# Six of eight experts taken in order of their load, each place with a capacity of its own

## The chip, the cores and the metric

One core of a Trainium2 chip. The metric is the device time of one execution in microseconds (us); lower is better. The kernel before takes 831.09 us in the median of three runs (829.47 to 831.78). About 0.3% of that, 2.5 us, is what a measurement of this kernel can tell from no change.

Engines are named as the profile names them: PE (TensorE; PEld is its weight load), DVE (VectorE), ACT (ScalarE), POOL (GpSimd) and SP (SyncE, whose queue issues most DMAs).

## What is computed

Three steps, each fed by the one before, all in float32:

```python
x = attention(q, k, v)              # 4 batches, 8 heads, 576 positions, 64 wide: a local window of 7
                                    # positions plus attention over means of 4; as rows: x is 2304 x 512
x = (silu(x @ w_gate) * (x @ w_val)) @ w_out        # hidden width 1536
xn, en = x / |x|, expert_emb / |expert_emb|
logits = xn @ en.T / tau                            # 8 experts
idx = argmax(logits, axis=1)                        # one expert for each row
out[idx == e] = gate[idx == e] * (relu(x[idx == e] @ w1[e]) @ w2[e])    # w1[e] 512 x 1024, w2[e] 1024 x 512
```

The last step is ragged: how many of the 2304 rows an expert gets is known only on the chip, when the last rows have been routed. For the input of the reference the eight counts are 297, 284, 329, 305, 296, 231, 280, 282.

## The kernel before, in words

**Products.** A float32 operand is split in two parts of a narrower float type (fp32r), hi and lo, and a product is three matmuls: hi by hi, hi by lo, lo by hi. ACT casts the hi part, DVE (now and then POOL) subtracts to get the lo part.

**Stages.** 16 pairs of heads (`heads`) feed the gated step, which runs over nine chunks of 256 rows (`gated`, `gemm1`, `gemm1p`, `gemm2`, `gemm2p`). The result rows go to a table in DRAM, `x2d`, and are routed chunk by chunk (`route`, `route_rows`, the last chunk in `last_m`): each row gets a slot number in its expert's stretch of two small tables `tabs`, which hold row number, gate and target. `base` holds the running counts. Behind the last chunk `last_base` works out whether an expert got more rows than its capacity.

**Experts.** They are taken in the order 0 to 7. Every expert has 336 columns (`CAP`, the sum of the tiles `SLT` = 128, 128 and 80 rows): the rows in its slots are gathered from `x2d` into three tiles (`load_slots` for experts 0 to 2, `load_groups` for the others), turned so that rows become columns, and padded with zeros. The first product (`l1`, line 1789) streams all 336 columns of an expert past the weights, 96 matmuls; the second one of experts 1 to 6 (`block_t`, line 1895) does the same, another 96, and `turn_out` (line 1855) turns the result back. The second product of expert 7 (`second`, `l2`, line 1799) goes tile by tile: for each of its three tiles 24 matmuls of 512 columns. Expert 0 begins early with two tiles (256 columns) and does its third one later (`rest_a`, `rest_b`). `send` and `finish` scatter the rows to `out`. Weights come in 64 loads of 512 KB on SP's queue (`load_experts`, lines 1604 and 1607) into a ring of 36 slots; ACT casts each (line 1587) and DVE subtracts (line 1590).

**Rows past a capacity.** Behind the last expert stands a branch on a register that is read from `ovm` (line 2105). Only if an expert got more than 336 rows are the rest computed there, tile by tile (`past_tile`).

**What sets the order.** All of it is listed by a planner (`Sched`): tasks ask for an engine with a duration and a priority, the lowest number first, and the planner writes each engine's instructions in the order in which it imagines them. On the chip each engine runs its list in order and waits by semaphores. The numbers are constants at the head of the file: `HEAD_P`, `REST_P`, `HALF_P` and others for the head pairs, `WEIGHT_P` and `PART_P` for the weights of the gated step, `LAT_DMA` for the time that the planner gives a DMA.

**The start.** Until the first chunk is there, `keep_warm` (line 432) fills PE with products of zeros, as many as the planner sees room for.

Of the kernel before, what the change touches and what calls it, by code (L numbers as in the profile page):

```python
# [30 lines left out]
E = 8  # L31
# [22 lines left out]
NCST = P + P // 2 + NPAIR * WK // 2 + 3 * E + 4 * NT18 + NOV  # L54
NEYE = P + P // 2
DMA_T = 700.0
NX = 3
# [22 lines left out]
def t_actp(n): return 65 + 0.815 * n  # L80
# [22 lines left out]
class Sched:  # L103
# [7 lines left out]
    LAT_DMA = 4302.0  # L111
# [154 lines left out]
HEAD_P = [-2.213, -0.549, -1.68, -1.811, 3.298, 3.164, 2.209, 4.92, 16.0, 17.0, 18.0, 19.0, 36.0, 37.0, 38.0, 39.0]  # L266
# [5 lines left out]
REST_P = [0.035, -0.34, 0.132, 3.049]  # L272
HALF_P = [0.772, -3.481, 2.169, -0.88]
VALUE_P = 1.076
PART_P = [-0.491, 0.188, 0.558]
CONST_P = 4.124
TAB_P = 14.361
EN_P = 0.664
# [7 lines left out]
WEIGHT_P = [1.117, 2.258, 4.696, 6.055, -10.334, 12.398]  # L286


def build(tc, a):
# [66 lines left out]
    past = take(NOV)  # L356
    tri = cst.tile([P, P], F32R, name="tri")
# [9 lines left out]
    ovm = cst.tile([P, 1], I32, name="ovm")  # L367

# [656 lines left out]
    def x_pair(c, k, xh, xl):  # L1025
        hi = -0.4
# [27 lines left out]
    def act_h(c, p, ps, j):  # L1054
# [3 lines left out]
        yield op("ACT", t_actp(CT), -0.5)  # L1058
        nc.scalar.activation(th, ps[:, 0:CT], AF.Tanh, scale=0.5)
        yield op("DVE", t_dve(CT), -0.5)  # L1060
        nc.vector.scalar_tensor_tensor(out=th, in0=th, scalar=1.0, in1=ps[:, 0:CT], op0=ALU.add, op1=ALU.mult)
        yield op("DVE", t_dve(CT), -0.5)
        nc.vector.scalar_tensor_tensor(out=th, in0=th, scalar=0.5, in1=ps[:, CT:2 * CT], op0=ALU.mult, op1=ALU.mult)  # L1063
        sc.put("ps", ps)
        yield op("ACT", t_act(CT), -0.5)
        nc.scalar.copy(hh[:, j].bitcast(F32R), th)  # L1066
        e = yield both(CT, -0.5)
# [50 lines left out]
    def act_half(c, u, i, pg, pv, hh, hl):  # L1118
# [4 lines left out]
        yield op("ACT", t_actp(CT), -0.5)  # L1123
        nc.scalar.activation(th, pg[:, r], AF.Tanh, scale=0.5)  # L1124
        yield op("DVE", t_dve(CT), -0.5)
# [6 lines left out]
        yield op("DVE", t_dve(CT), -0.5)  # L1132
# [5 lines left out]
        yield op("ACT", t_act(CT), -0.5)  # L1138
        nc.scalar.copy(hf, th)  # L1139
        e = yield both(CT, -0.5)  # L1140
# [263 lines left out]
    def last_base():  # L1404
        yield op("DVE", 75, -0.9, True)
        nc.vector.tensor_tensor(out=base, in0=base, in1=base0, op=ALU.subtract)
        yield op("DVE", 80, -0.9)
        nc.vector.tensor_reduce(out=ovc, in_=base, axis=AX.X, op=ALU.max)
        yield op("DVE", 75, -0.9)
        nc.vector.tensor_scalar(out=ovc, in0=ovc, scalar1=float(CAP), scalar2=0.0, op0=ALU.subtract, op1=ALU.max)  # L1410
        yield op("DVE", 75, -0.9)
        nc.vector.tensor_copy(ovm, ovc)

    def route_rows(c, m, row, lp):
# [9 lines left out]
        for e in range(NFIRST if c in FIRST_C else 0, E):  # L1424
            yield op("DVE", t_dve(DM) + 10, -0.3, "acc")
# [257 lines left out]
    def load_groups(e):  # L1683

        if e > 3:
            yield ("wait", ("xs", e - 2, 0))
# [536 lines left out]
```

## Time and profile before

| | |
|---|---|
| median of three runs | 831.09 us (829.47 to 831.78) |
| the profiled execution | 830.24 us, its span 828.4 us |
| PE busy | 816.2 us (99%) |
| DVE, ACT, POOL busy | 562.0, 372.6, 209.6 us |
| HBM read and written | 86.10 and 10.89 MB |

The span runs from the first to the last instruction; 1.84 us of the execution's own time lie around it. "Busy" of PE counts an instruction from its start to a modelled end, and the next one starts before that end: the time that a matmul costs in a row of them is the distance between two starts, not its duration. An engine's row of idle time names what ended it.

### The profile page before, as it was taken

To read this page: it belongs to the slowest core of one execution; us is meant where nothing else is said; L and a number is where in the kernel's file an instruction comes from. 1 tells how busy PE (TensorE), PEld (TensorE's weight loads), DVE (VectorE), ACT (ScalarE), POOL (GpSimd) and SP (SyncE) were. 2 spreads that over 40 slices of the span, in tenths; PEclk is the share of its full clock that TensorE was granted. 3 is DMA by queue.
4 is the path that set the end of the run, shared out by engine and by line. 5 is a ranking of instruction groups with operands and counts; after the bars stand their busy time and mean duration, and the time that the engine had idled before them with its cause. 6 is when DMAs were issued, how large, how long until landed. Compare 5 with 4: busy or idle time off the path is not lost. (4 is left out here: it accounts for less than half of the span.)

```text
span 828.4 us, 16139 instructions
## 1 busy us (share of the span) xinstructions
PE 816.2 (99%) x6155; PEld 715.9 (86%) x6161; DVE 562.0 (68%) x1450; ACT 372.6 (45%) x923; POOL 209.6 (25%) x221
## 2 busy tenths in 40 slices
PE   9989999999999999999999999999999999999997
PEld 5778778877787787787899999999999999999995
DVE  6999989678545577544699985766467675774510
ACT  3988788453223443223422323355346464454331
POOL 5562200010000100000123230123344734744111
PEclk9999999999999999999999999999999999999999
DMA  9983546222120230110432100454476555555100
GB/s 264 321 259 107 167 151 197 94 101 61 60 60 3 83 123 13 61 60 2 152 77 27 53 1 27 118 184 109 135 239 193 178 166 173 186 168 170 49 29 30
DMA packets 64049, 96.34 MB, mean 116 GB/s; under 512 B 14753, under 2 KB 33699, under 8 KB 63840
## 3 DMA queue, kind: packets, MB, share of 16 engines
q1 hardware_dynamic: 58688, 85.50, 33.5%
q0 software_dynamic: 4992, 9.51, 3.6%
q8 instruction: 49, 0.80, 0.4%
q14 instruction: 32, 0.26, 0.1%
q10 hardware_dynamic: 288, 0.26, 0.1%
HBM read 86.10 MB, written 10.89 MB: 117 GB/s over the span
## 5 line engine op out<-in xcount | busy, mean ns | idle before, releaser
L1165 PE MATMUL ps<-xb,w 128*128 128x512 f32 x512 | 173.6, 400 | 0.0
L1109 PE MATMUL ps<-xb,w 128*128 128x256 f32 x960 | 126.9, 284 | 0.0
L1789 PE MATMUL ps<-xh,w 128*128 128x336 f32 (+1 forms) x512 | 124.8, 316 | 0.5 <-issue 0.4
L1109 PEld LDWEIGHTS ps<-xb,w 128*128 128x128 f32 x960 | 121.4, 191 | 1.4 <-issue 0.2
L1165 PEld LDWEIGHTS ps<-xb,w 128*128 128x128 f32 x512 | 96.1, 188 | 22.6 <-issue 0.8
L1165 PE MATMUL ps<-xl,w 128*128 128x512 f32 x256 | 100.6, 393 | 0.0
L1789 PEld LDWEIGHTS ps<-xh,w 128*128 128x128 f32 x512 | 88.5, 188 | 2.2 <-DVE xl L1752 1.2
L1590 DVE TENSOR_TENSOR w<-w,w 128x1024 fp32r<-128x1024 f32 x64 | 77.1, 1219 | 10.2 <-ACT w L1587 7.4
L1789 PE MATMUL ps<-xl,w 128*128 128x336 f32 (+1 forms) x256 | 79.8, 312 | 0.0
L1775 DVE SCALAR_TENSOR_TENSOR el<-ps,eh 128x336 fp32r<-128x336 f32 (+1 forms) x62 | 30.0, 493 | 64.6 <-ACT eh L1773 60.1
L1730 POOL DMA_INDIRECT xs<-x2d,w x55 | 65.7, 1194 | 22.6 <-issue 14.9
L1773 ACT ACTIVATE eh<-ps 128x336 fp32r<-128x336 f32 (+1 forms) x62 | 27.7, 447 | 96.7 <-PE ps L1789 69.8
L1587 ACT CAST w<-w 128x1024 fp32r<-128x1024 f32 x64 | 65.9, 1049 | 0.0
L1165 PEld LDWEIGHTS ps<-xl,w 128*128 128x128 f32 x256 | 48.2, 188 | 8.5
L1895 PE MATMUL x<-eh,w 128*128 128x336 f32 x192 | 51.4, 317 | 0.0
L1895 PE MATMUL ps<-eh,w 128*128 128x336 f32 x192 | 51.3, 317 | 0.0
L1227 PE MATMUL x<-w,hh 128*128 128x512 f32 x160 | 50.4, 396 | 0.0
L1789 PEld LDWEIGHTS ps<-xl,w 128*128 128x128 f32 x256 | 48.3, 189 | 0.1
L1139 ACT CAST hh<-th 128x256 fp32r<-128x256 f32 x64 | 24.0, 408 | 41.4 <-DVE th L1133 41.3
L1126 DVE SCALAR_TENSOR_TENSOR th<-th,ps 128x256 f32<-128x256 f32 x64 | 23.9, 415 | 27.3 <-ACT th L1124 27.3
L1066 ACT CAST hh<-th 128x256 fp32r<-128x256 f32 x44 | 17.8, 406 | 52.8 <-DVE th L1063 52.3
L1197 PE MATMUL x<-w,hh 128*128 128x512 f32 x128 | 41.0, 401 | 0.0
(337 smaller groups left out, 1725.9 us busy)
## 6 DMA issues: line engine op xcount, KB each, us to landing
w<-w SPq DMA_DIRECT2D x64, 512.0 KB
w<-w_gate SPq DMA_DIRECT2D x10, 512.0 KB
w<-w_val SPq DMA_DIRECT2D x10, 512.0 KB
w<-w_out SPq DMA_DIRECT2D x10, 512.0 KB
aw<-qk SPq DMA_DIRECT2D x16, 291.0 KB
x2d<-sg SPq DMA_DIRECT2D x18, 256.0 KB
w<-qk SPq DMA_DIRECT2D x12, 291.0 KB
xl<-x2d SPq DMA_DIRECT2D x13, 256.0 KB
```

The lines of the kernel that those rows point to most:

```text
L1109: nc.tensor.matmul(ps[:, o:o + CT], ww[:, k, fs], xx[:, k, :], start=(k == 0 and n == 0), stop=(k == KD - 1 and n == 2))
L1139: nc.scalar.copy(hf, th)
L1165: nc.tensor.matmul(ps, ww[:, k, fs], xx[:, :, k], start=(k == 0 and n == 0), stop=(k == KD - 1 and n == 2))
L1197: nc.tensor.matmul(x2p[x], l, r[:, js], start=(u == 0 and n == 0), stop=(u == 2 * NFB - 1 and n == 2))
L1227: nc.tensor.matmul(x2p[c, m], l[:, j, ms], r[:, js], start=(p == 0 and j == 0 and n == 0), stop=(p == NFB - 1 and j == 1 and n == 2))
L1587: nc.scalar.copy(hi.bitcast(F32R), raw)
L1590: nc.vector.tensor_tensor(out=lo.bitcast(F32R), in0=raw, in1=hi.bitcast(F32R), op=ALU.subtract)
L1730: nc.gpsimd.indirect_dma_start(out=xs[:, n * P:(n + 1) * P], out_offset=None, in_=x2d.rearrange("t (a d) -> (t a) d", a=KD), in_offset=bas ...
L1773: nc.scalar.activation(hh[:, j, 0:n].bitcast(F32R), ps[:, 0:n], AF.Relu)
L1775: nc.vector.scalar_tensor_tensor(out=hl[:, j, 0:n].bitcast(F32R), in0=ps[:, 0:n], scalar=0.0, in1=hh[:, j, 0:n].bitcast(F32R), op0=ALU.max ...
L1789: nc.tensor.matmul(ps[:, 0:n], ww[:, k, fs], xx[:, k, 0:n], start=(k == 0 and t == 0), stop=(k == KD - 1 and t == 2))
L1895: nc.tensor.matmul(ys[d][:, 0:n], ww, h, start=(f == 0 and t == 0), stop=(f == NF2 - 1 and t == 2))
```

## The change

Experts 2 to 7 become six places. When all rows are counted, DVE ranks the six experts by their counts (`last_base`) and writes two things: which expert stands at which place (`ordi`) and which capacity each expert has got (`cape`). SP reads `ordi` into six registers (`set_order`), and the loads of weights and table rows for the places 2 to 7 take the expert's number from a register (`expert_of`, `tab_rows`). The places have 336, 312, 304, 288, 288 and 256 columns, the last one thus two tiles in place of three. Experts 0 and 1 keep 336. The branch behind the end compares each expert's count with its own capacity. The stretches of `tabs` have 2304 in place of 2384 slots.

Besides, the planner gets other numbers: the listing priorities of the head pairs, of the weights of the gated step, of routing and of a few elementwise steps, and 4951 in place of 4302 for a DMA's time.

```diff
-NOV = -(-(NTOK - CAP) // P)
-EST = CAP + NOV * P
 NSL = len(SLT)
 EARLY = 256
+FIXED = 2
+CAPS = (CAP, CAP, CAP, 312, 304, 288, 288, 256)
+SLTE = [tuple(m for m in (P, P, n - 2 * P) if m) for n in CAPS]
+NOV = -(-(NTOK - EARLY) // P)
+EST = EARLY + NOV * P
...
+ACT_P, XP_P, ROW_P, FIRST_P = -0.456, 0.525, -0.154, 30.295
...
-    LAT_DMA = 4302.0
+    LAT_DMA = 4951.0
...
-HEAD_P = [-2.213, -0.549, -1.68, -1.811, 3.298, 3.164, 2.209, 4.92, 16.0, 17.0, 18.0, 19.0, 36.0, 37.0, 38.0, 39.0]
+HEAD_P = [-2.038, -0.549, -1.624, -1.708, 2.951, 3.075, 1.758, 4.264, 14.859, 18.007, 17.102, 19.186, 33.984, 40.93, 39.946, 38.167]
...
     def last_base():
         yield op("DVE", 75, -0.9, True)
         nc.vector.tensor_tensor(out=base, in0=base, in1=base0, op=ALU.subtract)
...
+        nc.vector.scalar_tensor_tensor(out=key, in0=lo, scalar=-1.0 / 16, in1=base[:, FIXED:], op0=ALU.mult, op1=ALU.add)
...
+        nc.vector.tensor_tensor(out=rk2, in0=inner(key), in1=outer(key), op=ALU.is_gt)
...
+        nc.vector.tensor_reduce(out=rank, in_=rk2, axis=AX.X, op=ALU.add)
...
+        nc.vector.tensor_copy(ordi, val)
+        sc.set("order")
...
+        nc.vector.tensor_reduce(out=cape[:, FIXED:], in_=rk2, axis=AX.X, op=ALU.add)
...
+    def set_order():
+
+        yield ("wait", "order")
+        yield ("lag", 500)
+        for i in range(NRK):
+            turn[FIXED + i] = nc.values_load(ordi[0:1, i:i + 1], engines=[mybir.EngineType.SP], min_val=FIXED, max_val=E - 1,
+                                             skip_runtime_bounds_check_because="a permutation of the ranked experts")
+        sc.set("turns")
+
+    def expert_of(x, e):
+
+        return x[e] if e < FIXED else x[bass.ds(turn[e], 1)].rearrange("o r c -> (o r) c")
+
+    def tab_rows(t, e, lo, hi):
+        return expert_of(tabs[t].rearrange("(e s) w -> e s w", e=E)[:, lo:hi, :], e)
...
         for e in range(E):
+            if e == FIXED:
+                yield ("wait", "turns")
             for nm, dst in (("w1", w1s), ("w2", w2s)):
...
                         nc.sync.dma_start(out=raw.rearrange("p (k f) -> p k f", k=4),
-                                          in_=a["w1"][e, :, i * 256:(i + 1) * 256].rearrange("(p k) f -> p k f", p=P))
+                                          in_=expert_of(a["w1"][:, :, i * 256:(i + 1) * 256], e).rearrange("(p k) f -> p k f", p=P))
...
     def load_group(e, j, ix):
-        m = SLT[j]
+        m = SLTE[e][j]
...
-        n = sum(SLT[j] for j in tiles)
+        n = sum(SLTE[e][j] for j in tiles)
...
-            yield from expert(e, range(NSL), False, {1: lambda: rest_b(0, last)} if e == 1 else None)
+            yield from expert(e, range(len(SLTE[e])), False, {1: lambda: rest_b(0, last)} if e == 1 else None)
```

How the instruction lists of three engines read at the places that matter (names of buffers end in numbers; what is left of the arrow is written):

PE, expert 7: the end of a first product (`ps` <- `xh`, `xl`) and the first pieces of the second (`x`, `ps` <- weights, `eh`, `el`). Before:

```order
L1789 MATMUL ps_1_103<-xh_1_5596,w_10_7991 128x336
L1789 MATMUL ps_1_103<-xl_1_5598,w_10_7991 128x336
L1789 MATMUL ps_1_103<-xh_1_5596,w_10_7983 128x336
L1799 MATMUL x_1_110<-w_9_8118,eh_1_5599 128x512
L1799 MATMUL x_1_110<-w_9_8106,eh_1_5599 128x512
L1799 MATMUL x_1_110<-w_9_8118,el_1_5601 128x512
L1799 MATMUL x_1_109<-w_9_8118,eh_1_5599 128x512
L1799 MATMUL x_1_109<-w_9_8106,eh_1_5599 128x512
L1799 MATMUL x_1_109<-w_9_8118,el_1_5601 128x512
L1799 MATMUL ps_1_108<-w_9_8118,eh_1_5599 80x512
L1799 MATMUL ps_1_108<-w_9_8106,eh_1_5599 80x512
L1799 MATMUL ps_1_108<-w_9_8118,el_1_5601 80x512
```

Now:

```order
L1850 MATMUL ps_1_109<-xh_1_5604,w_10_8024 128x256
L1850 MATMUL ps_1_109<-xl_1_5606,w_10_8024 128x256
L1850 MATMUL ps_1_109<-xh_1_5604,w_8_8002 128x256
L1860 MATMUL x_1_115<-w_8_8138,eh_1_5607 128x512
L1860 MATMUL x_1_115<-w_9_8113,eh_1_5607 128x512
L1860 MATMUL x_1_115<-w_8_8138,el_1_5609 128x512
L1860 MATMUL x_1_114<-w_8_8138,eh_1_5607 128x512
L1860 MATMUL x_1_114<-w_9_8113,eh_1_5607 128x512
L1860 MATMUL x_1_114<-w_8_8138,el_1_5609 128x512
```

The first product is 256 columns wide in place of 336, and of the three results of the second product (128, 128 and 80 rows) the third one is gone. The same rows of the places 3 to 6 read 312, 304, 288 and 288 in both products; place 2 reads 336 as before.

SP's queue, around the loads of the second weight of expert 1 (128x2x512); 128x4x256 is the first weight of expert 2, or of place 2. Before:

```order
L1553 DMA x2d<-sg_1_102 128x512
L1607 DMA w_3_6107<-w 128x2x512
L2105 TENSOR_LOAD ovm
L2105 ISA x2
L1607 DMA w_6_6170<-w 128x2x512
L1698 DMA w_8_6179<-tab_86 32x11x4
L1698 DMA w_8_6179<-tab_87 32x11x4
L1704 DMA w_8_6179<-tab_86 128x3x4
L1704 DMA w_8_6179<-tab_87 128x3x4
L1607 DMA w_8_6225<-w 128x2x512
L1607 DMA w_3_6345<-w 128x2x512
L1604 DMA w_3_6386<-w 128x4x256
```

Now:

```order
L1609 DMA x2d<-sg_1_106 128x512
L1665 DMA w_3_6114<-w 128x2x512
L1665 DMA w_6_6178<-w 128x2x512
L1459 TENSOR_LOAD ordi x6
L1665 DMA w_7_6247<-w 128x2x512
L2167 TENSOR_LOAD ovm
L2167 ISA x2
L1665 DMA w_7_6341<-w 128x2x512
L1662 ISA
L1662 DMA w_3_6413<-w 128x4x256
L1698 ISA
L1698 DMA tb_6430<-tab_86 128x3x4
```

Six register loads of the order stand ahead of the last two loads of expert 1; an address step (ISA) stands before each DMA that names a place; and the four reads of the table for the next expert have moved behind the first load of place 2.

DVE, behind the last routing: `base` less its start is the counts; 128x1024 is the lo part of a weight, `el` that of expert 0's relu. Before:

```order
L1406 TENSOR_TENSOR base<-base,cn 128x8
L1775 SCALAR_TENSOR_TENSOR el_1_5602<-ps_1_107,eh_1_5600 128x256
L1408 TENSOR_REDUCE ovc<-base 128x1
L1590 TENSOR_TENSOR w_4_5788<-w_4_5806,w_6_5789 128x1024
L1410 TENSOR_SCALAR ovc<-ovc 128x1
L1775 SCALAR_TENSOR_TENSOR el_1_5602<-ps_1_108,eh_1_5600 128x256
L1412 CAST ovm<-ovc 128x1
L1590 TENSOR_TENSOR w_4_5816<-w_5_5847,w_4_5828 128x1024
L1590 TENSOR_TENSOR w_4_5878<-w_7_5880,w_4_5879 128x1024
L1590 TENSOR_TENSOR w_5_5886<-w_4_5901,w_5_5887 128x1024
```

Now:

```order
L1417 TENSOR_TENSOR base<-base,cn 128x8
L1836 SCALAR_TENSOR_TENSOR el_1_5610<-ps_1_108,eh_1_5608 128x256
L1423 SCALAR_TENSOR_TENSOR rk<-cn,base 128x6
L1646 TENSOR_TENSOR w_5_5796<-w_4_5814,w_5_5797 128x1024
L1425 TENSOR_TENSOR rk_92<-rk 128x36
L1836 SCALAR_TENSOR_TENSOR el_1_5610<-ps_1_111,eh_1_5608 128x256
L1427 TENSOR_REDUCE rk<-rk_92 128x6
L1646 TENSOR_TENSOR w_4_5823<-w_5_5859,w_4_5846 128x1024
L1429 TENSOR_TENSOR rk_92<-rk,cn 128x36
L1646 TENSOR_TENSOR w_6_5885<-w_5_5887,w_5_5886 128x1024
L1431 TENSOR_TENSOR rk_92<-rk_92,cn 128x36
L1646 TENSOR_TENSOR w_5_5894<-w_4_5907,w_5_5900 128x1024
```

The steps of the ranking (`rk`) stand in turn with weight splits and relu splits; `ordi` is written three rows further on, behind one more relu split.

## Rows read from the trace of the kernel before

**Rows 1.** The page: its first line and line 1.

```profile
span 828.4 us, 16139 instructions
PE 816.2 (99%) x6155; PEld 715.9 (86%) x6161; DVE 562.0 (68%) x1450; ACT 372.6 (45%) x923; POOL 209.6 (25%) x221
```

**Rows 2.** Stretches: PE, PEld, DVE, ACT, POOL busy us (count); granted clock, DMA share, GB/s.

```profile
0.00:100.00 100.00, 93.56 (x1256) 75.11 (x1263) 89.55 (x212) 74.76 (x221) 47.00 (x66) 1.00 0.72 227
400.00:500.00 100.00, 99.93 (x696) 93.15 (x695) 91.89 (x376) 28.14 (x78) 27.48 (x30) 1.00 0.21 51
600.00:700.00 100.00, 99.54 (x641) 96.91 (x640) 64.92 (x106) 50.00 (x81) 50.92 (x43) 1.00 0.62 191
```

**Rows 3.** The same view: one expert, from its predecessor's transposes back to its own.

```profile
701.62:732.88 31.26, 31.24 (x205) 30.94 (x204) 20.42 (x35) 15.22 (x25) 16.54 (x14) 1.00 0.56 175
```

**Rows 4.** What PE waited for: line, releaser; us in total, times, longest.

```profile
PE ps L1090 <- POOL xl L1048: 1.5, 1, 1.5
PE ps L1090 <- DVE w L480: 0.8, 1, 0.8
PE ps L836 <- DVE x L922: 0.7, 1, 0.7
```

**Rows 5.** PE in order of time: start us, us; 48 matmuls of 336 columns between these.

```profile
646.13 0.31 PE L1789 MATMUL ps<-xh,w 128*128 128x336 f32 x1
653.53 0.32 PE L1789 MATMUL ps<-xh,w 128*128 128x336 f32 x1
```

**Rows 6.** The same view: 24 matmuls of 256 columns between these two starts.

```profile
580.36 0.28 PE L1789 MATMUL ps<-xh,w 128*128 128x256 f32 x1
583.18 0.40 PE L1799 MATMUL x<-w,eh 128*128 128x512 f32 x1
```

**Rows 7.** The same view: 18 matmuls of 512 columns between these two starts.

```profile
814.77 0.63 PE L1799 MATMUL x<-w,eh 128*128 128x512 f32 x2
818.93 0.62 PE L1799 MATMUL ps<-w,eh 128*80 128x512 f32 x2
```

**Rows 8.** Groups of instructions: weight loads of the experts' first product; weight splits.

```profile
L1789 PEld LDWEIGHTS ps<-xh,w 128*128 128x128 f32 x512 | 88.5, 188 | 2.2 <-DVE xl L1752 1.2 <-issue 0.5 <-ACT sg L1859 0.3
L1590 DVE TENSOR_TENSOR w<-w,w 128x1024 fp32r<-128x1024 f32 x64 | 77.1, 1219 | 10.2 <-ACT w L1587 7.4 <-issue 1.9 <-DMA w<-tab 0.4
```

**Rows 9.** Line 2105, the one register load on SP: ns min/median/max, start.

```profile
L2105 SPq TENSOR_LOAD <-ovm x1: 476/476/476, 573.9 to 573.9; - x1
L2105 SPq FUSED_REGOPS  x1: 181/181/181, 574.4 to 574.4; - x1
```

**Rows 10.** The queue of SP, then PE, in order of time, around experts 1 and 2.

```profile
580.28 11.71 SPq L1607 DMA_DIRECT2D w<-w  x2
594.84 0.57 SPq L1604 DMA_DIRECT2D w<-w  x1
596.16 0.32 PE L1789 MATMUL ps<-xh,w 128*128 128x336 f32 x1
629.68 0.31 PE L1789 MATMUL ps<-xh,w 128*128 128x336 f32 x1
```

**Rows 11.** DVE in order of time, behind the last routing.

```profile
571.73 0.16 DVE L1406 TENSOR_TENSOR base<-base,cn 128x8 f32<-128x8 f32 x1
571.80 0.42 DVE L1775 SCALAR_TENSOR_TENSOR el<-ps,eh 128x256 fp32r<-128x256 f32 x1
594.03 0.49 DVE L1677 TENSOR_TENSOR xl<-ps,xh 128x320 fp32r<-128x320 f32 x1 [0.81 <-ACT xh L1675]
```

**Rows 12.** PE at the start, then POOL at the end, in order of time.

```profile
1.52 5.80 PE L432 MATMUL x<-w 128*128 128x512 bf16 x14 [1.52 <-POOL w L428]
7.15 0.30 PE L855 MATMUL ps<-um,eye 128*128 128x320 bf16 x1
820.14 0.97 POOL L1814 DMA_INDIRECT out<-sg,w  x1 [3.19 <-ACT sg L1806]
824.24 0.91 POOL L1814 DMA_INDIRECT out<-xs,w  x1 [3.13 <-ACT xs L1806]
```

More of the change, by code (lines that the diff above doesn't have):

```diff
@@ L356, in build @@
     past = take(NOV)
+    capr = take(NRK)
     tri = cst.tile([P, P], F32R, name="tri")
@@ L367, in build @@
     ovm = cst.tile([P, 1], I32, name="ovm")
+    cape = cst.tile([P, E], F32, name="cape")
+    rk = cst.tile([P, 4, NRK], F32, name="rk")
+    rk2 = cst.tile([P, NRK, NRK], F32, name="rk2")
+    ordi = cst.tile([P, NRK], I32, name="ordi")
+    nc.gpsimd.memset(cape, float(CAP))
     slots("w", wp, NW, [P, 1024], True)
@@ L1025, in x_pair @@
     def x_pair(c, k, xh, xl):
-        hi = -0.4
+        hi = XP_P
         t = []
@@ L1137, in act_half @@
             sc.put("ps", pv)
-        yield op("ACT", t_act(CT), -0.5)
+        yield op("ACT", t_act(CT), ACT_P)
         nc.scalar.copy(hf, th)
-        e = yield both(CT, -0.5)
+        e = yield both(CT, ACT_P)
         on[e].tensor_tensor(out=lf, in0=th, in1=hf, op=ALU.subtract)
@@ L1406, in last_base @@
         nc.vector.tensor_tensor(out=base, in0=base, in1=base0, op=ALU.subtract)
[L1407 to L1411, printed above, removed]
-        nc.vector.tensor_copy(ovm, ovc)
+        r0, lo = iota8[:, 0, 0:NRK], iota8[:, 0, FIXED:]
+        key, rank, val = rk[:, 0], rk[:, 1], rk[:, 2]
@@ new lines, in last_base @@
+        yield op("DVE", 110, -0.9, True)
+        nc.vector.tensor_tensor(out=rk2, in0=inner(rank), in1=outer(r0), op=ALU.is_equal)
+        yield op("DVE", 110, -0.9, True)
+        nc.vector.tensor_tensor(out=rk2, in0=rk2, in1=inner(lo), op=ALU.mult)
+        yield op("DVE", 100, -0.9)
+        nc.vector.tensor_reduce(out=val, in_=rk2, axis=AX.X, op=ALU.add)
+        yield op("DVE", 75, -0.9, True)
+        nc.vector.tensor_copy(ordi, val)
+        sc.set("order")
+        yield op("DVE", 110, -0.8, True)
@@ new lines, in last_base @@
+        nc.vector.tensor_reduce(out=ovc, in_=iota8[:, 1, :], axis=AX.X, op=ALU.max)
+        yield op("DVE", 75, -0.8, True)
+        nc.vector.tensor_scalar(out=ovc, in0=ovc, scalar1=0.0, scalar2=None, op0=ALU.max)
+        yield op("DVE", 75, -0.8)
+        nc.vector.tensor_copy(ovm, ovc)
+    turn = {}
+    def set_order():
[5 more added lines that the diff above has]
+        sc.set("turns")
@@ L1633, in load_slots @@
         js = slice(parts[0], parts[-1] + 1)
+        if e >= FIXED:
+            yield ("wait", "turns")
         for t in range(2):
@@ L1686, in load_groups @@
             yield ("wait", ("xs", e - 2, 0))
+        yield ("wait", "turns")
         if not gt:
@@ L1710, in load_groups @@
         if e > 2:
-            yield ("wait", ("gather", e - 1, NSL - 1))
-        for j in range(NSL):
+            yield ("wait", ("gather", e - 1, len(SLTE[e - 1]) - 1))
+        for j in range(len(SLTE[e])):
             sc.spawn(sc.cur.prio + 0.1 * j, load_group(e, j, ix))
@@ L1863, in free_turned @@
     def free_turned(e, ysb):
-        for j in range(NSL):
+        for j in range(len(SLTE[e])):
             yield ("wait", ("turned", e, j))
@@ L1901, in block_t @@
             xss_tb[e] = xss[e][2]
-            for j in range(NSL):
+            for j in range(len(SLTE[e])):
                 sc.spawn(NCHUNK * 10 + e + 0.1 * j, turn_out(e, j, ysb))
@@ L1976, in expert @@
                 continue
-            hs.update({2 * i + j: [[x[:, j, t * P:t * P + SLT[t]].bitcast(F32R) for t in tiles] for x in (hh, hl)] for j in range(2)})
+            hs.update({2 * i + j: [[x[:, j, t * P:t * P + SLTE[e][t]].bitcast(F32R) for t in tiles] for x in (hh, hl)] for j in range(2)})
             fs += [2 * i, 2 * i + 1]
```

79 lines of the change are left out of this document (48 added, 31 removed).

## Prediction

> **What bounds the kernel now.** I read the page's first lines, then stretches of time, then one expert, then single instructions of each engine at the places that the change touches. The span is 828.4 us and PE is busy for 816.2 of it [rows 1]; it idles for 12.2 us in all, and 6.4 of these lie in the first 100 us. In the experts PE is busy for 99.5 us of 100, and at 400 to 500 for 99.9, although DVE has 91.9 there [rows 2]. One expert, from its predecessor's transposes to its own, takes 31.26 us, PE 31.24 of them; DVE has 20.4, ACT 15.2, POOL 16.5, and the DMA engines are busy for 56% [rows 3]. The granted clock is 1.00 in each stretch shown, so the clock is at the higher of its two levels throughout and has nothing to give. So PE's instructions set the end, and time can go in two ways: by less work on PE, or by the few waits of the front.
>
> That PE is "busy" doesn't say that its columns set the pace: its weight loads are busy for 30.94 of the same 31.26 us [rows 3], 188 ns each [rows 8]. What a column is worth must come from starts. 48 matmuls of 336 columns lie between 646.13 and 653.53: 154.2 ns each [rows 5]. 24 of 256 columns lie between 580.36 and 583.18: 117.5 ns [rows 6]. 18 of 512 columns lie between 814.77 and 818.93: 231.1 ns [rows 7]. The first two differ by 36.7 ns for 80 columns, 0.459 ns a column, and 154.2/336 is 0.459 too: in this range the time is proportional to columns. The check: 192 x 154.2 ns is 29.6 us of the expert's 31.26; the rest are its transposes.
>
> The trace disagrees with a rule in the Trainium skill, page "TensorE: Matmul & The Clock Gate", section "Back-to-back issue gap": it says that in a stream of weight loads and matmuls the spacing is set by both, with 81 ns at 128 and 131 ns at 512 columns. Its slope of 0.13 ns a column would make an estimate of 36,864 x 0.13 + 24 x 131 ns = 7.9 us saved, and 823.2 us. The same section gives N/2.4 + 2.5 ns for an isolated warm matmul; an estimate by it is 15.4 + 24 x 0.216 = 20.5 us saved, and 810.6.
>
> **The work removed.** The places 3 to 6 are narrower by 24, 32, 48 and 48 columns, together 152, in 192 matmuls each (96 of either product): 152 x 192 = 29,184 columns. Place 7 is narrower by 80 in its 96 first-product matmuls: 7,680. Together 36,864 columns at 0.459 ns: 16.92 us. The third tile of expert 7 goes with 24 matmuls of 512 columns: 24 x 0.2311 = 5.55 us [rows 7]. Sum: 22.47 us, all of it on the engine that sets the end. The slope between 336 and 512 columns is smaller, 0.437 ns [rows 5, 7]; with it the sum would be 0.8 us less. I take 0.459, since the new widths lie between the two from which it comes.
>
> This comes in full only if the others keep pace. The tightest places are 5 and 6, where the stay falls to 31.26 - 48 x 192 x 0.459 ns = 27.0 us. DVE's 20.4 and POOL's 16.5 us fit; the DMA engines have 0.56 x 31.3 = 17.5 us of work [rows 3]. Weights are as many as before, so only the cushion shrinks.
>
> **The work added.** *Ranking.* DVE gets 11 small operations behind the last routing. Before, the step is at 571.73 (0.16 us) with a relu split of 0.42 us behind it [rows 11]. Now the steps up to `ordi` stand in turn with four weight splits of 1.22 us [rows 8] and two relu splits: 571.73 + 4 x 1.22 + 2 x 0.42 + 7 x 0.16 = about 579 us. What stands behind on DVE is late by at most 11 x 0.16 = 1.7 us. The nearest work that matters is the last split of the rows of expert 1, which ends at 594.52 [rows 11], 1.6 us ahead of PE's first use at 596.16 [rows 10]. Most of the new operations stand behind those which that chain needs, so I take nothing; without that cover it is 0.1 to 1.7 us, once.
>
> *The order on SP.* Six register loads. One took 476 ns and its arithmetic 181 ns [rows 9], so six take about 4 us, and the registers are there at 583. Their wait for `ordi` holds up the loads queued behind: the last two of expert 1's second weight, then all of places 2 to 7. In the kernel before, that queue stands at 580.28 for 11.7 us in the second weight's loads, waiting for ring slots; the first load of expert 2 went out at 594.84 and its first matmul began at 629.68 [rows 10], 34.8 us of lead. The 4 us fall into a time in which SP waits anyway: nothing. Should the ring be free earlier, they come off the lead, which is eight times as long.
>
> *Addresses from registers.* 70 DMAs of the places 2 to 7 get a step before them. No row shows it. Nearest are the 181 ns of arithmetic [rows 9] and the 0.57 us of a DMA [rows 10]; both for 70 are 53 us of SP in the six stays, 165 us. The bounds are 0 and that sum as long as SP keeps its lead. I take 0.
>
> *Table reads.* Those for the next expert stand behind the first load of place 2, so at about 595 instead of 576 us. The gathers that need them are for the expert two places on, a stay of 31 us later. I take 0; without that cover each gather would be late by its read, about a microsecond.
>
> *The end.* The last scatter carries 128 rows rather than 80. The rows have 0.97 us for a scatter of 128 and 0.91 for one of 80 [rows 12]: 0.06 us, nothing.
>
> **The new listing order in the front.** PE starts with 17 warming matmuls in place of 14; these 14 took 5.80 us [rows 12], so three more cost up to 1.24 us if the first real one at 7.15 [rows 12] could have started when it did. Against that stand the waits that another order might remove: 1.5, 0.8 and 0.7 us, 3.0 together [rows 4]. The longest waits for a split on POOL at L1048, and two of these move from POOL to DVE. No row bounds what a reorder may lose, so I take the same 3.0 us to either side and nothing in the middle, since the gain and the loss are of one size and neither is excluded.
>
> **The sum.** 830.24 (the profiled execution) - 22.47 = 807.77. That execution lies 0.85 us below the median of the runs, so the forecast for the median is 808.6 us. Downward, 3.0 for the front and 1.6 for the spread of runs: 804.0. Upward, 3.0 for the front, 0.8 for the slope and 0.7 for the spread: 813.1.
>
> **The rivals.**
>
> *Columns don't set the spacing.* If the weight loads hold the spacing at 154 ns until 256 columns are reached, the places 3 to 6 save nothing, and what is left is 80 x 96 x 0.459 = 3.5 plus 5.55 us: 822.0. For it: weight loads busy for 99% of an expert. Against it: 117.5 ns with the very same weight loads at 256 columns. Chance 0.03. The page named above would have it so; by the trace's three widths it doesn't hold here.
>
> *The front moves by more than 3 us.* The front has 6.4 us of idle PE and 5.8 us of warming, so a good order could give more, and a bad one cost about as much: 803 or 815. Chance 0.06, half each.
>
> *Another engine falls short at the narrow places.* If the stay of places 5 and 6 can't fall below that of a 336-column expert, 2 x 4.2 us come back: 817. Against it stand DVE's 20.4 us and DMA's 17.5 in 27. Chance 0.02.
>
> *SP becomes the bound, slower than before.* If the DMAs with register addresses hold SP for long, weights come late. SP must issue 70 of them in the six stays, which are then 6 x 31.26 - 22.5 = 165 us. It decides from 165/70 = 2.4 us each, against 0.75 us in the rows; with 2.8 us SP needs 196 us, and the end moves out by 31: 839. For it: no row has such a DMA. Chance 0.02.
>
> *The change doesn't do what it says.* The counts of the ranked experts are 329, 305, 296, 282, 280 and 231 against capacities of 336, 312, 304, 288, 288 and 256, so nothing overflows. Were a count counted otherwise, the late branch would load one expert again, 8 x 512 KB at 175 GB/s [rows 3], 24 us: 833. Chance 0.01.
>
> **How the numbers follow.** The forecast has 0.86, with the three small costs at nothing or under 2 us. Outside the range lie the front's large moves (0.06), and the other four rivals (0.08); with some of the forecast's own tail that is under 2 in 10. All cases but the last two are faster than 828.6, which is 0.3% (2.5 us) below the median, about what a measurement can tell from no change: faster 0.97. Between 828.6 and 833.6 lies nearly nothing but part of the last rival: 0.01. Slower: 0.02.
>
> **What would show it.** In the changed profile the starts of matmuls at 312, 304 and 288 columns should lie 143, 139.5 and 132 ns apart; the stays should read 31.3, 29.1, 28.4, 27.0 and 27.0 us; the last place should have two tiles in its second product; the register loads should stand at about 579 to 583 us; and PE should still be busy for over 99% of each stay. A wait of PE for a weight split, with SP as its source, would speak for the bound on SP; spacings of 154 ns at 288 columns would make the first rival right. If the stays are as said and the total is not, the difference lies in the front: the time at which expert 1 begins, 596.16 before [rows 10], would have moved.

## The result, and the profile after

The changed kernel takes 811.31 us in the median of four runs (809.04 to 812.90) against 830.28 for the kernel before in the same batch: a ratio of 0.9768, with a 95% interval of 0.9738 to 0.9798, or 19.0 us. In two more batches it took 815.03 (ratio 0.9806, 0.9788 to 0.9824) and 811.22 us (0.9754, 0.9732 to 0.9776). The forecast was 808.6, with a range of 804.0 to 813.1, so the sign and the size are right, some 3 us of the gain did not arrive, and in the second batch another 4 were missing. Where these went is what the experiments are about.

The page of the changed kernel, its first line and PE's:

```profile
span 808.9 us, 16198 instructions
PE 796.7 (98%) x6139; PEld 698.4 (86%) x6140; DVE 560.1 (69%) x1460; ACT 370.5 (46%) x923; POOL 190.8 (24%) x202
```

The span is 19.5 us shorter and PE's busy time as well [rows 1]: PE still sets the end. The stretches, with the columns of [rows 2]; the last two are stays of one place between two turnings, which answer to [rows 3]:

```profile
0.00:100.00 100.00, 94.03 (x1249) 74.77 (x1251) 84.72 (x199) 71.85 (x215) 44.36 (x64) 0.97 0.68 211
600.00:700.00 100.00, 100.00 (x668) 97.89 (x667) 65.08 (x113) 50.27 (x83) 50.58 (x39) 1.00 0.66 199
701.67:729.40 27.73, 27.73 (x206) 27.72 (x204) 19.01 (x32) 15.12 (x25) 14.44 (x12) 1.00 0.66 197
729.40:756.51 27.11, 27.03 (x206) 26.77 (x205) 17.14 (x26) 14.73 (x25) 11.41 (x11) 1.00 0.62 196
```

A stay between two turnings holds most of one place and the beginning of the next one's first product. They were 31.81, 31.32, 31.26, 31.27 and 31.26 us, and are 30.59, 28.78, 27.73, 27.11 and 26.28 (the forecast had 31.3, 29.1, 28.4, 27.0 and 27.0); PE is busy in all of each but for 0.08 us in the fourth. In the first 100 us the granted clock has a mean of 0.97, which was 1.00.

The spacing of matmuls of the new widths, from PE in order of time; between the two starts of a pair lie 24 matmuls, of 312 columns in the first pair, 304 in the second and 288 in the third:

```profile
664.47 0.30 PE L1850 MATMUL ps<-xh,w 128*128 128x312 f32 x1
667.90 0.32 PE L1956 MATMUL x<-eh,w 128*128 128x336 f32 x1
...
693.64 0.30 PE L1850 MATMUL ps<-xh,w 128*128 128x304 f32 x1
696.96 0.30 PE L1956 MATMUL x<-eh,w 128*128 128x312 f32 x1
...
736.25 0.30 PE L1850 MATMUL ps<-xh,w 128*128 128x288 f32 x1
739.43 0.29 PE L1956 MATMUL x<-eh,w 128*128 128x288 f32 x1
```

These are 142.9, 138.3 and 132.5 ns; the forecast was 143, 139.5 and 132.

The ranking and the order on SP: DVE in order of time (the counts, then `ordi`), the six register loads and the address steps on SP (ns min/median/max, first and last start), and the first load of place 2:

```profile
575.17 0.16 DVE L1417 TENSOR_TENSOR base<-base,cn 128x8 f32<-128x8 f32 x1
581.37 0.16 DVE L1435 CAST ordi<-rk 128x6 int32<-128x6 f32 x1
```

```profile
L1459 SPq TENSOR_LOAD <-ordi x6: 261/270/480, 581.6 to 583.4; - x6
```

```profile
L1662 SPq FUSED_REGOPS  x24: 37/46/56, 592.4 to 743.3; - x24
L1662 SPq MOVE w<-w x24: 29/29/42, 592.5 to 743.4; - x24
```

```profile
598.77 0.61 SPq L1662 DMA_DIRECT2D w<-w  x1
```

From the counts to `ordi` it is 6.4 us (forecast about 7), the six loads take 2.3 us (4), and an address step costs 46 + 29 ns in the median of the 24 shown, which would be 5 us of SP for all 70. The first load of place 2 goes out at 598.77 and its first matmul starts at 633.49: a lead of 34.7 us, against 34.8 before [rows 10].

**Where the 19.5 us come from**, by the instants of the two traces, in us (596.16 stands in [rows 10]; a turning begins at 638.49 before and at 642.30 after):

| stretch | before | after | difference |
|---|---|---|---|
| start to the first matmul of expert 1 | 596.16 | 599.98 | +3.8 |
| from there to the first turning | 42.33 | 42.32 | 0.0 |
| five stays between turnings | 156.92 | 140.49 | -16.4 |
| last turning to the end | 32.99 | 26.11 | -6.9 |

Behind the front the change brings 23.3 us, and the front takes 3.8 back. What PE waited for in the changed kernel (columns as in [rows 4]):

```profile
PE x L443 <- POOL w L439: 1.6, 1, 1.6
PE ps L847 <- DVE x L933: 1.5, 1, 1.5
PE ps L1120 <- ACT w L726: 1.0, 1, 1.0
PE ps L742 <- POOL w L734: 1.0, 1, 1.0
PE ps L1101 <- DVE w L491: 0.8, 1, 0.8
```

The wait for a split on POOL that stood first is gone. Of these five, the first is the start of the program (1.5 us in the kernel before, too) and the last stood there before [rows 4]; 1.5, 1.0 and 1.0 us are new. PE's time ahead of expert 1, before and after:

```profile
0.00:596.16 596.16, 589.64 (x4719) 497.35 (x4726) 438.16 (x1252) 270.99 (x755) 116.77 (x141) 1.00 0.34 106
0.00:599.98 599.98, 593.94 (x4728) 500.55 (x4730) 442.00 (x1267) 272.14 (x756) 106.67 (x132) 0.99 0.34 105
```

PE idles for 6.5 us there before and for 6.0 after: the front is longer not by waits but by 4.3 us of busy PE, at a granted clock of 0.99 in place of 1.00. (Three more warming matmuls are in it.)

### The profile page after: what moved, and what is told of

Same layout as the page of the kernel before. It is cut to its first block, busy times and chain, and to the rows that moved or that the text cites. A ratio compares the mean times of both kernels' runs of the same rounds, so it can differ in the third digit from the quotient of the medians.

```text
span 808.9 us, 16198 instructions
## 1 busy us (share of the span) xinstructions
PE 796.7 (98%) x6139; PEld 698.4 (86%) x6140; DVE 560.1 (69%) x1460; ACT 370.5 (46%) x923; POOL 190.8 (24%) x202
## 5 line engine op out<-in xcount | busy, mean ns | idle before, releaser
L1850 PE MATMUL ps<-xh,w 128*128 128x256 f32 (+4 forms) x512 | 113.6, 302 | 0.1
L1850 PEld LDWEIGHTS ps<-xh,w 128*128 128x128 f32 x512 | 85.6, 188 | 0.6 <-ACT sg L1920 0.3
L1850 PE MATMUL ps<-xl,w 128*128 128x256 f32 (+4 forms) x256 | 76.5, 299 | 0.0
L1836 DVE SCALAR_TENSOR_TENSOR el<-ps,eh 128x336 fp32r<-128x336 f32 (+4 forms) x62 | 28.8, 464 | 59.3 <-ACT eh L1834 58.9
L1791 POOL DMA_INDIRECT xs<-x2d,w x46 | 58.4, 1269 | 22.3 <-issue 12.5
L1834 ACT ACTIVATE eh<-ps 128x336 fp32r<-128x336 f32 (+4 forms) x62 | 26.3, 425 | 80.8 <-PE ps L1850 79.3
L1956 PE MATMUL x<-eh,w 128*128 128x336 f32 (+3 forms) x192 | 47.9, 305 | 0.0
L1956 PE MATMUL ps<-eh,w 128*128 128x336 f32 (+3 forms) x192 | 47.9, 305 | 0.0
L1135 ACT ACTIVATE th<-ps 128x256 f32<-128x256 f32 x64 | 21.1, 379 | 50.8 <-PE ps L1176 50.8
L1150 ACT CAST hh<-th 128x256 fp32r<-128x256 f32 x64 | 24.1, 407 | 40.8 <-DVE th L1144 40.6
```

The source lines that it names most:

```text
L1791: nc.gpsimd.indirect_dma_start(out=xs[:, n * P:(n + 1) * P], out_offset=None, in_=x2d.rearrange("t (a d) -> (t a) d", a=KD), in_offset=bas ...
L1834: nc.scalar.activation(hh[:, j, 0:n].bitcast(F32R), ps[:, 0:n], AF.Relu)
L1836: nc.vector.scalar_tensor_tensor(out=hl[:, j, 0:n].bitcast(F32R), in0=ps[:, 0:n], scalar=0.0, in1=hh[:, j, 0:n].bitcast(F32R), op0=ALU.max ...
L1850: nc.tensor.matmul(ps[:, 0:n], ww[:, k, fs], xx[:, k, 0:n], start=(k == 0 and t == 0), stop=(k == KD - 1 and t == 2))
L1956: nc.tensor.matmul(ys[d][:, 0:n], ww, h, start=(f == 0 and t == 0), stop=(f == NF2 - 1 and t == 2))
```

## The experiments

**Three questions first:** does the front lose by the new listing numbers, by the clock, or does the ranking lose somewhere? Four kernels ran in one batch (the kernel before: 831.88 us).

*a_old_order*, the change with the listing numbers of the kernel before:

```diff
...
-    LAT_DMA = 4951.0
+    LAT_DMA = 4302.0
...
-HEAD_P = [-2.038, -0.549, -1.624, -1.708, 2.951, ...]
+HEAD_P = [-2.213, -0.549, -1.68, -1.811, 3.298, ...]
...
```

> The changed kernel with the listing numbers (priorities and DMA time) of the kernel before; ranking, register addresses and narrower places stay. Theory 1: the 3.4 to 3.8 us that the changed kernel lost ahead of the experts belong to the new listing, and there to 6.8 us at the lower clock level (47.8 to 54.6 us), which an idle stretch of PE at 45.96 precedes. Then they come back: 807.5 us (811.31 - 3.8), granted clock 1.00 in 40 to 60, first matmul of expert 0 at 563.4 as before. Theory 2: the new listing costs them by its order, clock or not: the same time here. Rival, theory 3: ranking, register loads or register addresses cost them: then about 811 here, and the loss is seen behind 563 us.

*b_new_order*, the same edit the other way round: the kernel before with the new numbers.

> The kernel before with the listing numbers of the change and nothing else of it (336 columns, order 0 to 7, no ranking). Theories 1 and 2: slower than before by 3.4 to 3.8 us, 833.7 to 834.1, and by theory 1 with a granted clock of 0.50 for some 7 us between 45 and 56. Theory 3: as before, 830.3.

*c_fill*, warming matmuls in PE's list where it waits at 45.96 (ahead of the eighth block of line 847):

```diff
...
+        blocks.append(n)
+        if len(blocks) == 8:
+            for _ in range(7):
+                nc.tensor.matmul(warm[0], identb, umask[:, 0:512], start=True, stop=True)
```

> The changed kernel with seven warming matmuls of 512 columns (1.5 us of work whose result nobody reads) in PE's list just where it waits from 45.96 to 47.48 us. Theory 1: if that idle stretch is what the clock falls for, the granted clock stays at 1.00 and the lost 3.4 us come back although more is computed: 807.9 us. Theory 2: about 811.3, or some tenths more, and the clock may do what it likes. Should the clock fall all the same, at the same place or later, the idle stretch is not what decides, and the time stays at 811.

*d_all336*:

```diff
-CAPS = (CAP, CAP, CAP, 312, 304, 288, 288, 256)
+CAPS = (CAP,) * 8
```

> The changed kernel with 336 columns in each place: new listing, ranking, register loads and register addresses are all there, only the narrower places are gone. If these cost nothing behind 563 us (forecast): the time of the changed kernel plus the 22.5 us worked out for the columns and tiles, 833.8; with the 23.3 us that the two traces differ by from the first turning back on, 834.6. Theory 3 with a loss that the narrow places hide or make: another sum, over 835 or under 833.

Measured: a 810.69 us (ratio 0.976, 0.973 to 0.979), b 832.19 (1.0001, 0.9988 to 1.0013), c 811.20 (0.9777, 0.9744 to 0.9809), d 831.56 (0.9993, 0.9979 to 1.0008).

*Theory 1, the clock, does not explain the loss by itself.* The clock of a_old_order in 40 to 50 and 50 to 60 us:

```profile
40.00:50.00 10.00, 8.66 (x162) 7.15 (x159) 9.99 (x22) 9.97 (x32) 6.46 (x7) 0.84 0.84 260
50.00:60.00 10.00, 10.00 (x111) 9.46 (x110) 9.22 (x20) 6.69 (x23) 5.09 (x6) 0.81 0.95 293
```

and of the changed kernel:

```profile
40.00:50.00 10.00, 8.40 (x163) 6.74 (x161) 9.97 (x22) 9.14 (x26) 4.34 (x6) 0.89 0.74 229
50.00:60.00 10.00, 10.00 (x85) 9.90 (x81) 9.03 (x20) 8.08 (x26) 3.10 (x3) 0.77 0.99 335
```

The clock falls as much in both, yet in a_old_order expert 1 starts at 596.53, as in the trace of before (596.16) that had no fall. DVE is busy for 19 of these 20 us; that PE at the lower level does there what it would else have spent waiting fits this, but is not shown by itself. In c_fill the wait was filled and the clock stayed at 1.00 from 40 to 60. But the fall did not go away; it stands later:

```profile
80.00:90.00 10.00, 8.02 (x56) 7.59 (x55) 6.91 (x17) 6.38 (x22) 5.15 (x4) 0.83 0.18 54
```

Expert 1 started at 599.65 all the same. So c_fill tells little, and a share of the clock stays open, since each trace with the new numbers has a fall, and among those with it at 40 to 60 expert 1 starts later where it is longer. The changed kernel in its third batch (told below) has the shorter one:

```profile
40.00:50.00 10.00, 8.20 (x171) 6.76 (x170) 9.97 (x21) 9.14 (x24) 4.36 (x6) 0.99 0.82 249
50.00:60.00 10.00, 10.00 (x78) 10.00 (x77) 10.00 (x22) 8.84 (x30) 2.56 (x3) 0.84 0.97 321
```

Where the mean of these 20 us is 0.915, as here and in four more traces with the new numbers, expert 1 starts at 598.5 to 599.2; where it is 0.83, as in the changed kernel's first trace and in that of s2 (below), at 600.0 and 599.6; where the fall stands at 80 to 100 (c_fill, g_static, h_256), at 599.7 to 601.9. With the old numbers the start does not go with the fall: 596.1 and 596.2 us without one, 595.6 at 0.915 and 596.5 at 0.825. About 1 us of the 3.8 can so be the clock's.

*Theory 2, the order, holds for the front.* Expert 1 starts at 596.16, 596.53, 595.55 and 596.07 us in the four traces with the old numbers (two of them of runs told below) and between 598.50 and 601.85 in ten with the new ones: 3.5 us later by the means, and 3.0 to 3.6 us later where traces with the same clock from 40 to 60 are compared. That b is nevertheless no slower has to do with the stays. With 336 columns they take 31.26 us in the kernel before and 30.99 in b and d; d's, as an example:

```profile
703.48:734.46 30.98, 30.98 (x205) 30.96 (x204) 20.32 (x34) 15.50 (x27) 17.30 (x14) 1.00 0.59 177
```

In the kernel before, 0.28 us go between the third and the fifth matmul behind a turning (seen in two stays; the others are as long), and 0.5 more in the first stay: 156.92 us for the five, against 154.93 in d. With the old numbers and narrow places only the first stay still has some of it (30.9 against 30.6 us), so it does not belong to the listing numbers alone. There is one trace of the kernel before; why the gaps are in it was not looked for.

*Theory 3 falls for d*: with ranking, registers and all address steps, but without narrower places, it is at 0.9993 of the kernel before. From d to the changed kernel (trace to trace, from expert 1's first matmul to the end) it is 230.31 to 208.92 us, -21.4; that is the narrowing alone.

**The end** is longer than forecast. POOL's last scatter in the changed kernel, and in d_all336:

```profile
803.81 0.97 POOL L1875 DMA_INDIRECT out<-xs,w  x1 [3.15 <-ACT xs L1867]
```

```profile
825.29 0.91 POOL L1875 DMA_INDIRECT out<-xs,w  x1 [3.14 <-ACT xs L1867]
```

From the end of that instruction to the end of the span it is 4.12 us (808.9 - 804.78), and in d 3.30 (829.5 - 826.20); the kernel before has 3.25. The instruction itself costs 0.06 us more, as [rows 12] said; but what it started has to land. The last tile now holds 103 rows (231 - 128). It held 26 (282 - 256) in the kernel before and none in d, where the last place has 231 rows as well and the third tile begins at 256. What the scatter's queue moved from there to the end (packets, MB, share of the engines), in the kernel before, d and the changed kernel:

```profile
q0 software_dynamic: 64, 0.05, 5.4%
q0 software_dynamic: 64, 0.00, 0.9%
q0 software_dynamic: 80, 0.21, 13.3%
```

Between d and the changed kernel, the columns and the tile gave 21.4 + 0.8 = 22.2 us, and the end took 0.8. That pair is at the upper end: over all traces of this document it is 3.8 to 4.2 us, 3.9 in the mean, in the eleven with 103 rows, 3.2 and 3.5 in the two with 26 rows (the kernel before and b_new_order) and 3.3 in d. So the end takes about 0.5 us, and not in proportion to the bytes, since 26 rows cost about as much as none. Some of it is no landing: a step of POOL's own behind the scatter takes 416 ns in the kernel before and 667 in the changed one.

```profile
L2105 POOLq INC_SWDGE_SEM  x1: 416/416/416, 825.2 to 825.2; - x1
L2167 POOLq INC_SWDGE_SEM  x1: 667/667/667, 804.8 to 804.8; - x1
```

**Does the price of a column carry on, and does the machinery cost anything?** A second batch (the kernel before: 830.28):

*after_again*, the changed kernel once more.

> The changed kernel as it stands, timed again beside the others of this batch. By the sum of terms as the traces now have it (columns and the third tile -22.3, a longer end +0.9, the rest within 1 us): 20.5 to 21.4 us under the kernel before. By the forecast's sum: 22.5 under it. If single runs lie 3 to 6 us over the rest, as in two of the variants, they are the changed kernel's own and not those variants'.

*g_static*, constants in place of ranking and registers:

```diff
...
-            turn[FIXED + i] = nc.values_load(ordi[0:1, i:i + 1], ...)
+        turn.update({FIXED + i: x for i, x in enumerate((2, 3, 4, 7, 6, 5))})
...
-        return x[e] if e < FIXED else x[bass.ds(turn[e], 1)].rearrange("o r c -> (o r) c")
+        return x[e] if e < FIXED else x[turn[e]]
```

> The changed kernel without ranking and without registers: the experts stand in the order of the known counts (2, 3, 4, 7, 6, 5) as constants, so the six register loads, the 70 address steps and the ranking on DVE are gone and the capacities of the experts are constants too. If the machinery costs nothing (forecast): the same as the changed kernel in this batch, within 1 us, first matmul of place 2 and the turning points as there. Rival: the loads with register addresses or SP's wait for the order use up the lead of the weights in some runs; then this one is faster by 1 to 3 us in the median and its slowest runs are gone.

*h_256*, which leaves out the rows of an expert past 256:

```diff
-CAPS = (CAP, CAP, CAP, 312, 304, 288, 288, 256)
+CAPS = (CAP, CAP, CAP) + (256,) * 5
...
-        nc.vector.tensor_scalar(out=ovc, in0=ovc, scalar1=0.0, scalar2=None, op0=ALU.max)
+        nc.vector.tensor_scalar(out=ovc, in0=ovc, scalar1=0.0, scalar2=None, op0=ALU.mult)
```

> The changed kernel with 256 columns in each of the places 3 to 7 and the late branch never taken: rows past 256 of an expert are left out. It asks how far the column price of 0.459 ns carries. If PE's columns stay the bound: 168 columns fewer in 192 matmuls, 14.8 us, and four turnings less in each of four places, 1.6 us: 16.4 us under the changed kernel of this batch, 794.9; a stay of 23.5 us with PE over 99% busy. If weights or another engine bound the narrow places (DMA has 17.5 us and DVE 20 us of work for one): stays of over 24.5 us, PE waiting for splits or casts, and 797 or more.

*a_again*, as a_old_order.

> The changed kernel with the listing numbers of the kernel before, once more. In its first trace expert 0 began 3.1 us earlier than in the changed kernel, and 1.8 us were lost again between 626 and 636. If that loss belongs to the listing: the same time as the changed kernel, within 1 us, and the same loss in the trace. If it was that run's alone: 1.5 to 3 us under the changed kernel, 808 to 809.5.

Measured: 815.03 us (0.9806, 0.9788 to 0.9824), 815.90 (0.9818, 0.9799 to 0.9837), 794.78 (0.9556, 0.9535 to 0.9577) and 812.06 (0.9785, 0.9758 to 0.9813).

h_256 came out at 794.78, next to the 794.9 that were worked out from the changed kernel's first 811.3 (by the words of the expectation, from the 815.03 of this batch, it would have been 798.6). That the two agree within 0.2 us is in part chance: between the traces of h_256 and of the changed kernel, 17.3 us are gone behind expert 1's start where 16.4 were expected, and that start comes 1.9 us later. Two of its stays:

```profile
697.81:721.27 23.46, 23.46 (x203) 23.46 (x202) 18.36 (x31) 13.24 (x22) 13.19 (x10) 1.00 0.80 225
721.27:744.75 23.48, 23.48 (x203) 23.48 (x202) 16.78 (x24) 13.36 (x22) 7.96 (x6) 1.00 0.69 213
```

They are 23.5 us, as said, and PE never waits, so nothing else bounds the narrow places even at 256 columns; the DMA engines are at 80% and 69%. g_static gained nothing over after_again: no sign there either that the machinery costs time, and its absence does not help against what is new in these two. In both, one stay is 4 to 5 us longer. After_again, where the changed kernel had 27.11:

```profile
728.86:761.07 32.21, 29.48 (x207) 28.25 (x206) 17.15 (x26) 14.74 (x25) 10.98 (x11) 0.95 0.50 165
```

PE inside it, each with the idle time ahead of it, and then ACT:

```profile
741.48 0.29 PE L1956 MATMUL x<-el,w 128*128 128x288 f32 x1 [0.30 <-issue]
742.20 0.39 PE L1956 MATMUL x<-eh,w 128*128 128x288 f32 x1 [0.43 <-issue]
742.91 0.29 PE L1956 MATMUL ps<-el,w 128*128 128x288 f32 x1 [0.19 <-issue]
...
745.74 0.40 PE L1956 MATMUL ps<-eh,w 128*128 128x288 f32 x1 [1.11 <-issue]
```

```profile
742.24 0.41 ACT L1834 ACTIVATE eh<-ps 128x288 fp32r<-128x288 f32 x1 [6.37 <-remote]
```

The same operation of ACT in the changed kernel's first trace:

```profile
738.04 0.41 ACT L1834 ACTIVATE eh<-ps 128x288 fp32r<-128x288 f32 x1 [1.63 <-PE ps L1850]
```

Nothing that the profile shows holds PE ("issue"): it starts one matmul or a few every 0.7 us from 740.8 to 745.7, and the clock falls behind it. ACT has waited since 735.9 for a product whose last matmul ended at 737.45, and it starts 4.8 us behind that end; in the changed kernel's first trace the same matmul ends at 738.01 and ACT starts 0.03 us behind it. ("remote" says that the profile finds no instruction that sent the signal when it came.) So PE's signals were late while its matmuls still came at their usual pace. DVE and ACT have next to nothing to do in this stretch, POOL issues its gathers as in the first trace, and the DMA engines are busy for 15% of it: no other engine is seen to fall short. The same pattern, worth 1.8 and 3.5 us, stands in both traces of the version with the old numbers, from 628 to 631 us in a_old_order and from 624 to 630 in a_again:

```profile
624.00:628.00 4.00, 2.88 (x14) 2.04 (x13) 1.57 (x4) 0.00 (x0) 3.08 (x4) 1.00 0.17 52
628.00:632.00 4.00, 2.89 (x18) 2.70 (x18) 0.98 (x3) 1.72 (x4) 0.92 (x1) 1.00 0.61 183
```

14 and 18 matmuls in 4 us, where the trace without the stretch (below) has 28. That version therefore started expert 1 3 us earlier and lost half of it here in one trace and all of it in the other, which goes with its measuring hardly better.

**What makes PE issue slowly?** The page counts 49 packets of instructions with 0.80 MB in one queue:

```profile
q8 instruction: 49, 0.80, 0.4%
```

PE has 12,279 matmuls and weight loads, so if these are its own, a packet holds some 250. The Trainium skill ("Runtime: NRT & Kernel Launch", section "Instruction fetch mechanics") has instructions come in blocks of 256 by DMA, mostly hidden; the size agrees with 49 packets, and no row here shows a block that comes late. In after_again this queue has one packet from 737 to 738.5 us, in time (16.7 us behind the one before it, 16.4 in the changed kernel's first trace), and none from there to 759, with the slow stretch in between; in g_static it is the same.

```profile
q8 instruction: 1, 0.02, 3.7%
```

So a block that comes late is not seen in these two. In the two traces with the old numbers a packet does start next to the stretch or in it (626.3 and 627.2 us), and takes 0.93 us. Still, that the place in PE's list matters can be tested: lengthen PE's list ahead of everything and see whether the slow stretch moves. In a third batch (the kernel before: 831.40), *after_third* is the changed kernel; *s2* and *s3* are

```diff
-            nc.tensor.matmul(ps, zb[:, 0:P], zb, start=True, stop=True)
+            for q in range(2):
+                w = slice(q * 512 // 2, (q + 1) * 512 // 2)
+                nc.tensor.matmul(ps[:, w], zb[:, 0:P], zb[:, w], start=True, stop=True)
```

and the same with three parts.

> The changed kernel once more, as the control of this batch. In its second timing (815.03 in the median) a trace showed what the first one (811.31) did not: from 741 to 746 us, in place 5, PE issues a matmul every 0.7 us with nothing to wait for, and that stay takes 32.2 us in place of 27.1. If this is the chip's or the batch's mood: 811 or 815 here, with or without such a stretch.

> The changed kernel with each warming matmul split in two halves: the same work, but PE's list is 86 instructions longer ahead of everything else (43 of them pairs of weight load and matmul). Theory 4: the stretch of slow issue comes when PE's instructions, which are fetched in blocks of about 250, run short, and where in the program that is depends on how the list falls into the blocks. Then the stretch stands elsewhere than in the control of this batch (about 86 instructions, 2.7 us, earlier within a place, or in another place), or it is gone and the time falls to 810 to 811. Rival, theory 5: it belongs to the place of the program (the narrow place with its DMAs and casts). Then it stands at the same matmuls as in the control, in the first third of place 5, and the times are alike.

> The same with three parts of each warming matmul, 172 instructions more than in the changed kernel. Theory 4: again another position, 172 instructions or some 5.5 us earlier than in the control, or none. Theory 5: as in the control.

Measured: 811.22 (0.9754, 0.9732 to 0.9776), 810.60 (0.9753, 0.9729 to 0.9778) and 810.39 us (0.9745, 0.9718 to 0.9773). None of the three traces has a slow stretch, the control's neither: nothing was told apart here. So the last kernel, *a_s2*, makes the same edit to the version that had shown the stretch in both its traces.

> The narrow places with the listing numbers of the kernel before, and each warming matmul in two halves, which puts 86 instructions more ahead in PE's list. Without the halves both traces of that version have a stretch of slow issue at 625 to 631 us, in the second product of expert 1, worth 1.8 and 3.5 us. Theory 4 (how PE's list falls into the blocks in which it is fetched): the stretch is gone from there or stands elsewhere; if gone, the first turning comes 44.1 us after expert 1's first matmul at most 42.4, and the median falls to 807.5 to 809. Theory 5 (it belongs to that place of the program): a stretch in the same matmuls and 810.5 to 812.

Measured: 807.74 us in the median of six runs (806.64 to 809.19), against 830.67; ratio 0.9715, interval 0.9688 to 0.9741. The same two windows as of a_again:

```profile
624.00:628.00 4.00, 4.00 (x28) 4.00 (x27) 3.20 (x7) 3.30 (x5) 3.21 (x3) 1.00 0.83 271
628.00:632.00 4.00, 4.00 (x28) 4.00 (x27) 1.96 (x3) 0.78 (x2) 1.49 (x1) 1.00 0.74 234
```

The stretch is gone, from expert 1's first matmul to the first turning it takes 42.35 us again (a_again: 45.83), and all six runs lie under the fastest of a_again (809.46), though two of a_old_order's six had 808.70 and 808.79. It has the lowest time of the versions that compute every row: narrow places, the old listing numbers, and a longer head of PE's list. By the trace it is longer by 80 instructions, not 86: the old numbers have 40 warming matmuls, now in 80 halves, and the new ones 43.

That the place of the instructions in PE's list decides is not shown. a_s2 ran in a batch of its own, without the unsplit version beside it, and the changed kernel lost its stretch from the second batch to the third with no edit at all. The traces speak for the batch as a rival: in each of the eight of the first two batches, 18 to 24 of PE's some 520 signals have no record within 0.4 us of the end of their matmul; in the three of the third batch and in a_s2 each one has. Four of those eight show a slow stretch, none of these four. (It is not the batch alone: the changed kernel's first trace has all of its signals, and that of the kernel before lacks 21.) The chip alone is not it, since a_again and a_s2 ran on the same one. What makes PE issue slowly stays open.

## Why the prediction was right, and where it was off

- **Columns set PE's pace**: right. 0.459 ns a column gave the three new spacings within 1.2 ns, and at 256 columns in five places stays of 23.5 us, as expected. The first rival would have had 154 ns at 288 columns; 132.5 were measured. The rule of the Trainium skill ("TensorE: Matmul & The Clock Gate", "Back-to-back issue gap") that led to 823 us does not agree with these rows. The prediction's second estimate, 810.6, is nearer to 811.3 than the forecast, but by chance: it has 20.5 us for the removed work, where the traces have 22.2.
- **The work removed**: 22.47 us forecast, 22.2 found between two traces that differ in nothing else.
- **Ranking, register loads, addresses, table reads at nothing**: right (d at 0.9993, g_static no faster than after_again). The rival that SP becomes the bound needed 2.4 us for each DMA; an address step takes 0.075 and the DMA behind it 0.54.
- **The end at 0.06 us**: the step that was off is "nothing" for the last scatter. It priced POOL's instruction and left out all that follows it to the end of the span: about 0.5 us by all traces, 0.8 in the pair above.
- **The new listing order at nothing, with 3.0 us to either side**: mis-sized. It costs some 3.5 us at expert 1's start, of which about 1 can be the clock's. The waits that it removes are replaced by others, and the time goes to a longer busy PE, so that counting PE's waits could not show the loss. Two us come back behind it, because the gaps of 0.28 us behind each turning went away; the prediction had not seen these, since it took the 31.26 us of a stay for pure work. That the time lay within the range owes something to luck: the front alone lost more than the 3.0 us allowed, and the gaps, which nobody had counted, gave two back.
- **"PE's clock has nothing to give"** was read from one execution. Others fall to the lower level for some us in the front; with the old numbers expert 1 starts no later for it, with the new ones about 1 us later where the fall is longer.
- **PE's slow issue** was no rival at all. The nearest, "another engine falls short at the narrow places", has the right size for one of its two places (4 to 5 us at place 5), and no engine is seen to fall short there.
- The sum of terms as measured: -22.2 for the narrowing, +0.5 for the end, +3.5 for the front, -2.0 for the gaps, together -20.2; the changed kernel's first and third timings have -19.0 and -20.2, with intervals of some 2 us to either side, and its second (-15.3) has the slow stretch of some 5 us besides.

## What to carry to other kernels

Where one engine is busy throughout, price a change by the distance between starts of the same instruction at two sizes; that held here to 1% over widths that had not been measured. A last transfer is priced to the end of the span, not to the end of the instruction that starts it. And a change that bundles work removed with a new order of instructions is worth taking apart: here the first was worth 22 us, and the second cost 3 us in the front. Whether a version without it is faster as a whole rests on a_s2 alone, 3 us under the changed kernel in another batch, with intervals that overlap. A version that is to show a cause needs its control in the same batch.

## What was not expected of the hardware

PE can issue a matmul or two every 0.7 us for 3 to 6 us with nothing to wait for, while ACT gets the signal of a product 4.8 us behind its last matmul; one and the same program shows this in one batch and not in two others. The granted clock of one program differs from run to run: 0.990 to 0.999 on the mean of a run, in six runs of a_old_order. It goes with the time: of the kernel before on one chip, the eleven executions with a mean of 0.997 or more took 829.2 to 830.7 us, the nine with 0.992 to 0.996 took 831.6 to 835.8; which of the two brings the other is not shown. And in the front, where DVE is busy for 19 us of 20, a mean clock of 0.825 over 20 us left no trace in expert 1's start with the old numbers (596.53 against 596.16).
